# Which PSUM banks the two expert products and the token transposes share in an attention, experts and dense network kernel

## The chip, the cores and the metric

One Trainium2 chip, one core of it. The metric is the device time of one execution in microseconds (us); the kernel before is given by the median of three runs.

## What is computed

The reference is three networks in a row; only the middle one is touched by the change:

```python
x = attention(q, k, v)                  # 4 batches x 576 rows, 8 heads of 64: x is 2304 x 512
expert_idx = np.argmax(x @ w_gate, axis=1)          # one of 8 experts for each token
for e in range(E):
    xe = x[expert_idx == e]
    h = np.maximum(xe @ w1[e], 0.0)     # first product, 512 -> 1024
    ye = h @ w2[e]                      # second product, 1024 -> 512
    out[mask] = gate_w[mask, None] * ye
h = np.maximum(out @ w_in, 0.0)         # dense network, 512 -> 2048 -> 512
y = (h * h) @ w_out
```

## The kernel before

Attention runs first (to about 170 us of the span), then the experts, then the dense network. The tokens are sorted by expert with indirect DMAs, and the experts are worked in order of size: expert 0 is the largest, expert 7 the smallest, with at most 384, 384, 352, 352, 304, 256, 256 and 224 tokens. Two blocks of expert 0 are worked early, under the end of attention. Below, "expert 1" is the second in this order.

Every fp32 number is carried as two fp16 halves, so each product has three passes. For one expert, with `n` tokens:

- **First product** (`s1`, L789 to L799): eight groups, here called group 0 to group 7, one for each 128 of the 1024 hidden features. A group is 12 matmuls into one PSUM bank (L795 to L797). It is evicted in two steps: ScalarE (ACT) writes the high half of the ReLU (L798), then VectorE (DVE) reads the bank again and writes the low half (L799). The bank is free after that second step.
- **Turns** (`turn`, L989, and `transpose_x`, L782): the gathered token rows of the NEXT expert are transposed, up to 128 rows at a time, by eight TensorE transposes into one bank (L786), and copied out by ACT (L787). An expert has two or three turns, called turn 0 to turn 2. They are issued after groups 3, 5 and 7.
- **Second product** (`s2`, L840 to L856): four accumulators, one bank each, 96 matmuls in all (L849 to L851), over the eight hidden groups. At the end ACT copies the four banks into `yT` (L854).

While an expert runs, its engines also make ready what comes later. The weights of the next expert come by DMA in chunks of 128x1024 fp32, and each is split in two fp16 halves by ACT (L769) and DVE (L770). The dense network's weights are decoded and split in steps (`wide`): L871 to L873, L894 to L897 and L903 or L919 on DVE, L902 or L918 on ACT.

PSUM has eight banks of 128x512 fp32. The pool gives them to four tags of two banks each, a, b, c and d. A new tile of a tag takes one of its two banks, and its first matmul waits until the tile that held that bank has been read out. The tags before the change:

- first product: a, b, a, b, ... by group (L791);
- turns: d (L784);
- second product: c, c, a, b for its four accumulators (L843);
- the dense network's banks (`bank`, L1161): a, b, c in turn, or a and b alone while `self.narrow` is true, which it is in expert 6's second product and from the fourth of nine blocks of the dense network on (L1054, L1416). In expert 7 the first seven products of the dense network (`wide1(0, 0)`, L1058) run ahead of the second product, with a, b and c.

Each engine executes its own list of instructions in order. The recording layer (Tile) sets these lists: it reorders what the code issues by its own priorities, puts the semaphore waits in, and picks which of a tag's two banks a tile gets. A change of tags therefore moves instructions on all engines.

## Time and profile before

| what | us |
|---|---|
| median of three runs | 748.76 (748.24 to 751.16) |
| the profiled execution | 754.0, of which its span is 752.2 |
| PE (TensorE) busy | 711.6, 95% of the span |
| DVE busy | 594.4, 79% |
| ACT busy | 442.9, 59% |
| POOL busy | 212.0, 28% |

The profile comes from one execution. "PE busy" counts matmuls whose ends are modelled, and back-to-back matmuls overlap in it, so a wait shows better in the idle time before an instruction than in the busy share. "Idle before <-X" names the instruction whose end released the waiting one.

### The profile page before, as it was taken

To read this page: it belongs to the slowest core of one execution; us is meant where nothing else is said; L and a number is where in the kernel's file an instruction comes from. 1 tells how busy PE (TensorE), PEld (TensorE's weight loads), DVE (VectorE), ACT (ScalarE), POOL (GpSimd) and SP (SyncE) were. 2 spreads that over 40 slices of the span, in tenths; PEclk is the share of its full clock that TensorE was granted. 3 is DMA by queue.
4 is the path that set the end of the run, shared out by engine and by line. 5 is a ranking of instruction groups with operands and counts; after the bars stand their busy time and mean duration, and the time that the engine had idled before them with its cause. 6 is when DMAs were issued, how large, how long until landed. Compare 5 with 4: busy or idle time off the path is not lost. (4 is left out here: it accounts for less than half of the span.)

```text
span 752.2 us, 19605 instructions
## 1 busy us (share of the span) xinstructions
PE 711.6 (95%) x7979; PEld 600.8 (80%) x7979; DVE 594.4 (79%) x1454; ACT 442.9 (59%) x748; POOL 212.0 (28%) x247
## 2 busy tenths in 40 slices
PE   5989899999988999999899999999999999999996
PEld 5889799788755666788798566777899999999995
DVE  5888788864788999969987987868678787878672
ACT  5878788852466655657544342435657575757561
POOL 4493522335353401000000346533411111111011
PEclk9999999989999999999999999999999999999998
DMA  8798203765899887467713000000000000000000
GB/s 329 289 379 186 80 30 53 294 152 178 221 300 319 281 264 233 131 212 239 233 48 127 17 16 15 2 30 1 30 2 30 2 30 2 30 2 30 2 30 29
DMA packets 35656, 91.71 MB, mean 122 GB/s; under 512 B 5209, under 2 KB 13547, under 8 KB 35547
## 3 DMA queue, kind: packets, MB, share of 16 engines
q1 hardware_dynamic: 29803, 75.77, 31.6%
q0 software_dynamic: 5760, 14.65, 5.9%
q8 instruction: 64, 1.05, 0.6%
q14 instruction: 29, 0.24, 0.1%
HBM read 77.54 MB, written 13.04 MB: 120 GB/s over the span
## 5 line engine op out<-in xcount | busy, mean ns | idle before, releaser
L1178 PEld LDWEIGHTS <-wi 128*128 128x128 f16 x3024 | 170.6, 98 | 4.3 <-issue 3.1
L1315 PEld LDWEIGHTS <-wr 128*128 128x128 f16 x1008 | 98.1, 98 | 12.1 <-issue 0.7
L1201 ACT CAST wr<-work 128x1024 f16<-128x1024 f32 (+1 forms) x72 | 59.9, 832 | 58.3 <-DVE work L1207 41.6
L1178 PE MATMUL ps_a<-work,wi 128*128 128x128 f16 x1344 | 84.2, 219 | 0.0
L1178 PE MATMUL ps_b<-work,wi 128*128 128x128 f16 x1272 | 79.7, 219 | 0.4 <-ACTq L1066 0.4
L1202 DVE TENSOR_TENSOR wr<-work,wr 128x1024 f16<-128x1024 f32 (+1 forms) x72 | 70.3, 1000 | 4.4 <-ACT wr L1201 4.4
L310 PE MATMUL ps_a<-yT,wr 128*128 128x192 f32 (+2 forms) x288 | 64.9, 346 | 6.9 <-DMA wr<-in_q_dram 4.8
L322 ACT ACTIVATE pb<-pb,nm 128x192 f32<-128x192 f32 (+2 forms) x144 | 56.1, 433 | 14.8 <-DVE nm L315 14.1
L1343 POOL DMA_INDIRECT out_dram<-o,oid x18 | 25.6, 1423 | 101.4 <-ACT o L1341 66.8
L769 ACT ACTIVATE wr<-rw 128x1024 f16<-128x1024 f32 x40 | 42.2, 1057 | 19.5 <-DMA rw<-in_w_dram 18.9
L1278 POOL TENSOR_TENSOR yT<-wr 128x512 f32<-128x512 f16 x8 | 11.2, 1401 | 148.3 <-ACTq L1066 117.1
L310 PEld LDWEIGHTS ps_a<-yT,wr 128*128 128x128 f32 x288 | 45.6, 200 | 8.2 <-DMA yT<-in_k_dram 7.0
L315 DVE CUSTOM_DVE_ANT_0 pb<-ps_a,bias 128x192 f32<-128x192 f32 (+2 forms) x144 | 44.1, 326 | 9.9 <-PE ps_a L310 7.8
L770 DVE SCALAR_TENSOR_TENSOR wr<-rw,wr 128x1024 f16<-128x1024 f32 x40 | 48.8, 1220 | 3.6 <-ACT wr L769 3.4
L1210 ACT ACTIVATE work<-work 128x1024 f32<-128x1024 f32 x24 | 25.4, 1058 | 37.7 <-DVE work L1198 37.7
L333 PE MATMUL ps_b<-cst,pb 128*128 128x128 f32 x256 | 43.9, 283 | 0.7 <-ACT pts L337 0.7
L795 PE MATMUL ps_a<-work,wr 128*128 128x352 f16 (+4 forms) x112 | 33.7, 301 | 5.4 <-ACT yT L854 3.9
L778 POOL DMA_INDIRECT xg<-xd,idx x21 | 25.8, 1227 | 36.8 <-PE ps_d L786 27.7
L849 PE MATMUL ps_c<-work,wr 128*128 128x352 f16 (+5 forms) x128 | 35.9, 283 | 0.3 <-DVE work L1198 0.3
L851 PE MATMUL ps_c<-work,wr 128*128 128x352 f16 (+5 forms) x128 | 35.9, 283 | 0.0
L850 PE MATMUL ps_c<-work,wr 128*128 128x352 f16 (+5 forms) x128 | 35.9, 283 | 0.0
L1227 DVE TENSOR_TENSOR work<-work 128x512 f32<-128x512 f32 x18 | 13.0, 725 | 28.7 <-ACT work L1195 28.7
(308 smaller groups left out, 2009.5 us busy)
## 6 DMA issues: line engine op xcount, KB each, us to landing
rw<-in_w_dram SPq DMA_DIRECT2D x40, 512.0 KB
wi<-in_w_dram SPq DMA_DIRECT2D x20, 512.0 KB
rw<-in_wo_dram SPq DMA_DIRECT2D x16, 512.0 KB
rw<-in_wi_dram SPq DMA_DIRECT2D x32, 256.0 KB
wr<-in_q_dram SPq DMA_DIRECT2D x14, 512.0 KB
xd<-xhl POOLq DMA_DIRECT2D x16, 256.0 KB
yT<-in_k_dram SPq DMA_DIRECT2D x7, 576.0 KB
rw<-in_v_dram SPq DMA_DIRECT2D x12, 325.0 KB
```

The source lines that it names most:

```text
L310: nc.tensor.matmul(ps[:, s, first:hi], q[g, u, hh // 4][:, hh % 4, s if u < 4 else 0, :], self.kt[g, hh // 2][:, hh % 2, key0:key0 + hi - ...
L315: self.last_ttr = nc.vector.tensor_tensor_reduce(out=pb[:, s, first:hi], in0=ps[:, s, first:hi], in1=self.bias[:, hh, first - lo:192], sca ...
L322: self.last_exp = nc.scalar.activation(pb[:, s, first:hi], pb[:, s, first:hi], AF.Exp, bias=nm[:, s:s + 1], scale=-1.0)
L333: nc.tensor.transpose(pt[:, t, :, s, :], pb[:, s, t * P:(t + 1) * P], self.idf)
L769: self.nc.scalar.activation(t[:, 0], st, AF.Copy, scale=sc)
L770: self.nc.vector.scalar_tensor_tensor(t[:, 1], st, sc, t[:, 0], op0=ALU.mult, op1=ALU.subtract)
L849: nc.tensor.matmul(py, wh, hh, start=fc == 0, stop=False)
L850: nc.tensor.matmul(py, wl, hh, start=False, stop=False)
L1178: self.nc.tensor.matmul(ps[:, j], w[:, kp, a, w0 * P:(w0 + 1) * P], v[:, 2 * x + kp], start=kp + b == 0, stop=kp == 1 and b == 2)
L1201: self.end_act = self.fin_act = nc.scalar.copy(hi, src)
L1202: self.end_dve = self.fin_dve = V.tensor_tensor(lo, src, hi, op=ALU.subtract)
L1315: nc.tensor.matmul(ps[n], x[:, v, j], y[j][:, w], start=m + i + j == 0, stop=m == 1 and i == 2 and j == 3)
```

## The change

Three edits. The second product takes its accumulators from c, c, d, d. The turns take the banks of the first product: turn 0 from b, turn 1 from a, turn 2 from b. The dense network's products in expert 7 stay on a and b, and the dense network's own stage starts again with a, b and c.

```diff
-    def transpose_x(self, xg, dst, copy=None):
+    def transpose_x(self, xg, dst, copy=None, tag='d'):
         n = xg.shape[0]
-        pt = self.psum("d", [P, 8, P], F16)[:, :, :n]
+        pt = self.psum(tag, [P, 8, P], F16)[:, :, :n]
...
     def s2(self, ws, hts, at, n, then=None):
-        ys = [self.psum(t, [P, n]) for t in "ccab"]
+        ys = [self.psum(t, [P, n]) for t in "ccdd"]
...
-                self.transpose_x(g, xt[:, :, c * P:c * P + g.shape[0]], nc.scalar.copy)
+                self.transpose_x(g, xt[:, :, c * P:c * P + g.shape[0]], nc.scalar.copy, 'bab'[c])
...
-            self.narrow = e == 6
+            self.narrow = e >= 6
...
         nrm = {1: self.norm(1, 7168, None)}
+        self.narrow = False
         next(nrm[1])
```

How the instructions stand after it, at the two places on which the prediction rests.

On PE in expert 4 (groups of 304 tokens), the first matmuls that wait, before the change. In order: group 0, group 2, group 3, turn 0, group 4, group 5, turn 1, group 6, group 7:

```order
L795 MATMUL ps_a<-work,wr 128x304 [waits Activation_49]
...
L795 MATMUL ps_a<-work,wr 128x304 [waits Activation_49]
...
L795 MATMUL ps_b<-work,wr 128x304 [waits Activation_49]
...
L786 MATMUL ps_d<-id_131,xg 128x128 [waits PE_49]
...
L795 MATMUL ps_a<-work,wr 128x304 [waits DVE_49]
...
L795 MATMUL ps_b<-work,wr 128x304 [waits DVE_49]
...
L786 MATMUL ps_d<-id_131,xg 128x128 [waits PE_49]
...
L795 MATMUL ps_a<-work,wr 128x304 [waits DVE_49]
...
L795 MATMUL ps_b<-work,wr 128x304 [waits DVE_49]
```

The same place after it: group 0, group 1, turn 0, group 5, group 6, group 7:

```order
L795 MATMUL ps_a<-work,wr 128x304 [waits Activation_49]
...
L795 MATMUL ps_b<-work,wr 128x304 [waits PE_49]
...
L786 MATMUL ps_b<-id_131,xg 128x128 [waits DVE_49]
...
L795 MATMUL ps_b<-work,wr 128x304 [waits DVE_49]
...
L795 MATMUL ps_a<-work,wr 128x304 [waits DVE_49]
...
L795 MATMUL ps_b<-work,wr 128x304 [waits Activation_49]
```

Groups 2 and 3 wait for nothing now, and turn 0, which had a bank of its own, waits for DVE. By the bank that each gets, turn 0 waits for group 1's second eviction step, group 5 for group 3's, group 6 for group 4's, and group 7 for ACT's copy of turn 0. Before, groups 4, 5, 6 and 7 waited for groups 0, 1, 2 and 3. Experts 2, 5 and 6 are like expert 4; experts 1, 2 and 3 also have a turn 2, which waits for group 5's. In experts 1 and 3 the layer gives group 5 the bank of turn 0, so that it waits for ACT's copy; in expert 1 group 6 in the same way gets the bank of turn 1.

On DVE in expert 1 (384 tokens), a stretch of the difference, from group 3's eviction on:

```order
 L919 SCALAR_TENSOR_TENSOR wi_3346<-dec,wi_3346 128x512
+L799 SCALAR_TENSOR_TENSOR work<-ps_b,work 128x384
 L799 SCALAR_TENSOR_TENSOR work<-ps_a,work 128x384
+L871 TENSOR_SCALAR dec<-rw 128x512
 L770 SCALAR_TENSOR_TENSOR wr<-wi_3343,wr 128x1024
-L871 TENSOR_SCALAR dec<-rw 128x512
+L872 SCALAR_TENSOR_TENSOR dec<-rw,dec 128x512
 L799 SCALAR_TENSOR_TENSOR work<-ps_b,work 128x384
-L872 SCALAR_TENSOR_TENSOR dec<-rw,dec 128x512
+L873 SCALAR_TENSOR_TENSOR dec<-rw,dec 128x512
```

Group 3's low half (the first L799 row) stood six rows earlier, ahead of three weight splits (L770), and now stands behind them. In experts 2, 3 and 4 some evictions move in this way by one to four rows; from expert 5 on DVE's list is the same as before.

## Rows read from the trace of the kernel before

**Rows 1.** Busy time by stage: experts 1 to 7, one row each, from group 0 on.

```profile
core 0: us, PE busy (x) PEld busy (x) DVE busy (x) ACT busy (x) POOL busy (x), PEclk, DMA share, GB/s
197.00:235.70 38.70, 34.33 (x221) 20.72 (x219) 30.12 (x47) 20.79 (x32) 18.28 (x23) 0.96 0.91 302
235.70:269.50 33.80, 31.68 (x217) 20.61 (x216) 32.37 (x67) 22.79 (x33) 9.91 (x10) 0.95 0.86 283
269.50:301.10 31.60, 30.12 (x218) 19.85 (x216) 29.06 (x53) 18.82 (x29) 3.92 (x3) 1.00 0.79 245
301.10:326.90 25.80, 25.80 (x210) 19.67 (x208) 21.27 (x37) 15.99 (x25) 0.00 (x0) 1.00 0.41 134
326.90:350.10 23.20, 22.20 (x211) 19.73 (x209) 17.66 (x31) 13.53 (x23) 0.00 (x0) 1.00 0.77 245
350.10:376.30 26.20, 22.78 (x220) 19.86 (x218) 25.09 (x47) 16.22 (x29) 0.00 (x0) 1.00 0.75 238
376.30:404.80 28.50, 28.16 (x362) 27.64 (x360) 25.79 (x45) 11.83 (x26) 0.00 (x0) 1.00 0.09 29
```

**Rows 2.** Who PE waited for, 150 to 410 us: total, times, longest.

```profile
PE ps_a L795 <- ACT yT L854: 3.9, 3, 2.1
PE ps_d L786 <- DMA xg<-xd,idx: 3.4, 1, 3.4
PE ps_a L1131 <- DVE sd L1126: 2.3, 1, 2.3
PE ps_a L795 <- DVE work L799: 1.5, 2, 0.8
PE ps_b L849 <- DVE work L799: 1.3, 2, 1.0
PE ps_c L849 <- DVE work L1198: 0.3, 1, 0.3
```

**Rows 3.** PE's order of time in expert 2: group 2, turn 0, second product's first matmul.

```profile
241.55 0.31 PE L795 MATMUL ps_a<-work,wr 128*128 128x352 f16 x1 [2.12 <-ACT yT L854]
...
246.81 0.61 PE L786 MATMUL ps_d<-id,xg 128*128 128x128 f16 x8
...
255.20 0.32 PE L849 MATMUL ps_c<-work,wr 128*128 128x352 f16 x1
```

**Rows 4.** The stretch behind that wait; columns as in rows 1.

```profile
241.50:247.00 5.50, 5.45 (x28) 3.14 (x28) 5.50 (x17) 4.01 (x7) 2.88 (x3) 0.69 0.79 256
```

**Rows 5.** DVE's evictions L799: expert 2's group 1; group 4 of experts 2 to 6.

```profile
246.86 0.52 DVE L799 SCALAR_TENSOR_TENSOR work<-ps_b,work 128x352 f16<-128x352 f32 x1
...
252.77 0.51 DVE L799 SCALAR_TENSOR_TENSOR work<-ps_a,work 128x352 f16<-128x352 f32 x1
...
284.13 0.52 DVE L799 SCALAR_TENSOR_TENSOR work<-ps_a,work 128x352 f16<-128x352 f32 x1
...
313.54 0.47 DVE L799 SCALAR_TENSOR_TENSOR work<-ps_a,work 128x304 f16<-128x304 f32 x1
...
339.26 0.42 DVE L799 SCALAR_TENSOR_TENSOR work<-ps_a,work 128x256 f16<-128x256 f32 x1
...
362.56 0.42 DVE L799 SCALAR_TENSOR_TENSOR work<-ps_a,work 128x256 f16<-128x256 f32 x1
```

**Rows 6.** PE: the first matmul of group 6 in experts 1 to 6.

```profile
214.66 0.33 PE L795 MATMUL ps_a<-work,wr 128*128 128x384 f16 x1
...
251.28 0.31 PE L795 MATMUL ps_a<-work,wr 128*128 128x352 f16 x1
...
282.80 0.31 PE L795 MATMUL ps_a<-work,wr 128*128 128x352 f16 x1
...
311.42 0.29 PE L795 MATMUL ps_a<-work,wr 128*128 128x304 f16 x1
...
336.50 0.27 PE L795 MATMUL ps_a<-work,wr 128*128 128x256 f16 x1
...
360.23 0.27 PE L795 MATMUL ps_a<-work,wr 128*128 128x256 f16 x1
```

**Rows 7.** ACT: the copy of turn 1 in expert 1.

```profile
217.48 1.00 ACT L787 COPY work<-ps_d 128x1024 f16<-128x1024 f16 x1
```

## The prediction

> **What bounds the kernel now.** I read the stage table first, then the list of PE's waits, then the order of time on PE, DVE and ACT around those waits. The change touches experts 0 to 7, and of these experts 1 to 6 carry the price. In the stage table [rows 1] the reader is to see how full DVE is beside PE: it is busy for 30.12 of 38.70 us in expert 1 (78%), 96% in expert 2, 92% in expert 3, 82% in expert 4, 76% in expert 5 and 96% in expert 6. PE runs most of these stages without a pause, but no engine has much room.

> The list of waits [rows 2] is to show what the two edits can remove. PE stands 3.9 us, in three pieces, before a group of the first product until ACT has copied an accumulator of the second product out of a bank of tag a (L854). It stands 1.3 us, in two pieces, in the second product until DVE has evicted a group of the first (L849 behind L799). The 3.4 us for the gathered rows, the 2.3 us for the norm's small matrices (L1126) and the 1.5 us of L795 behind L799 have other causes and are not removed. The order of time shows the largest piece: group 2 of expert 2 starts at 241.55 after 2.12 us [rows 3].

> **What goes.** With accumulators in c and d, both kinds of wait lose their cause: 3.9 + 1.3 = 5.2 us. One piece has a tail. [...] Groups 2 and 3 took 246.81 - 241.55 = 5.26 us [rows 3], while groups 6 and 7 of the same expert, with a turn of some 0.36 us, took 255.20 - 251.28 = 3.92 us [rows 3, 6], 1.78 a group. The tail cost 5.26 - 3.56 = 1.7 us. So the credit is 5.2 us, or 6.9 with the tail.

> [...] I leave tails out of the sum, since expert 3, which holds the second piece of the 3.9 us, stands at a clock of 1.00 throughout [rows 1].

> **What comes in its place.** The turns no longer have banks of their own. A turn and two groups share a pair of banks, and the distance between a bank's use and its next use shrinks. Before, group 6 needed group 2's eviction, with groups 3, 4, 5 and two turns in between. Now it needs group 4's, with only group 5 and turn 1 in between, some 2 us. Likewise turn 0 needs group 1's, group 5 needs group 3's.

> How late are evictions? Rows 5 give DVE's time for group 4 in experts 2 to 6 and rows 6 the start of group 6. The eviction of group 4 ends at 253.28, 284.65, 314.01, 339.68 and 362.98 (start plus duration); group 6 started at 251.28, 282.80, 311.42, 336.50 and 360.23 [rows 5, 6]. If DVE's list ran at the same times, group 6 would start later by 2.0, 1.85, 2.6, 3.2 and 2.75 us. What follows it on PE (group 7, turn 2, the second product) would move with it, because each of those is ready on time.

> In expert 1, group 6 gets the bank of turn 1 and needs ACT's copy of it, which ends at 217.48 + 1.00 = 218.48 [rows 7] against a start at 214.66 [rows 6]: 3.8 us. The new order has nine matmuls of the second product ahead of group 6. At 0.16 us each they fill 1.5 us of that, so 2.3 is left; 1.0 of it is the longest piece of the second product's own wait [rows 2], which is no longer met there. I take 1.3.

> The removed waits do not return as credit in these figures. In expert 2, group 2 may start 2.12 us earlier, but turn 0 then needs group 1's eviction, which ends at 246.86 + 0.52 = 247.38 [rows 5], and turn 0 started at 246.81 [rows 3]. The gap moves from group 2 to turn 0. Behind it stand the same groups and the same tail. The late one after ACT's copies is DVE.

> **The smaller parts.** In expert 0, the transposes of its last block now wait for ACT's copy of an accumulator of tag d, and an eviction stands behind the copy of a turn; such a copy takes 1.00 us [rows 7], so the two cost at most 2. They are hidden: expert 1's turn 0 waits 3.4 us for a gather [rows 2], whose DMA does not depend on PE there. Without that cover they would cost those 2 us. In expert 7, the dense network's seven products have four banks for six. The wait of 0.3 us for a bank of tag c goes [rows 2], and two products come just behind an eviction of the first product; I take -0.3, with 0 to +1 as the other end. On POOL and on SP's queue only gathers and loads that are early by many us change places with their neighbours: nothing.

> **The sum.** Its ends lie far apart, because a lag of PE need not reach the end of its stage, nor the next one.
> - Upper end: every lag is passed on in full. 1.3 + 2.0 + 1.85 + 2.6 + 3.2 + 2.75 = 13.7 us.
> - Lower end: no lag, credit alone: -5.2, with the tail -6.9.
> - The value: a lag is passed on where DVE's list itself waits for PE, since then the next evictions and weight splits are late as well. DVE's share says where that is. In experts 2, 3 and 6 (96, 92 and 96%) DVE goes on with weights whatever PE does and finds PE's groups waiting: a lag there is caught up, as DVE sets the stage's end. In experts 1, 4 and 5 (78, 82 and 76%) it has room, waits, and carries the lag on: 1.3 + 2.6 + 3.2 = 7.1. Expert 6 gives some back: PE's 2.3 us on the norm [rows 2] shrink when PE comes later. I take 2.1 of them, near all, as DVE is at 96% there and does not move with PE: 7.1 - 2.1 = 5.0. The 0.3 of expert 7 stays inside that figure's error.

> The profiled execution took 754.0 us with a span of 752.2; the sum makes it 759.0. That execution is 5.2 us above the median of the runs shown, so on the median, 748.8, the change gives **753.8 us**, 0.7% slower.

> **The rivals.**
> 1. *The lags never arise* (faster). Without waits at groups 2 and 3, PE hands its first groups over earlier, ACT and DVE evict earlier, and the short distance is enough. It gives 748.8 - 5.2 = 743.6. It decides where group 4's eviction ends within some 2 us of the group's end. For it: the copies L854 no longer hold anything up. Against it: in expert 4, which had no wait of that kind, the eviction still came 2.6 us too late for the new distance. [...] Chance 0.18.
> 2. *All is caught up* (no change). DVE and the weight loads set the end of each stage, so PE's new waits only fill time in which it would have waited at the next place. For it: three stages with DVE above 90%. Against it: experts 4 and 5. Removing 1, 4 and 5 but for 0.5 gives 749.3. Chance 0.27.
> 3. *Every lag adds up*, with the moved evictions on DVE (group 3's of expert 1 now behind three weight splits) on top of nothing else: 748.8 + 13.7 = 762.5, if DVE waits for PE in all stages. Against it: the shares of 92 to 96%. Chance 0.10.

> My forecast has 0.45, of which 0.05 lies within the bound of no change.

> **How the numbers follow.** About 0.5% (3.7 us) is what a measurement of this kernel can tell from no change. Slower by more: 0.40 + 0.10 = 0.50. Within: 0.27 + 0.05 = 0.32. Faster by more: 0.18. The range of 8 in 10 runs from 744.5 to 760.5: below lies about half of rival 1, above most of rival 3. As cases of both signs hold much of the chance, the forecast's own range is 751.5 to 757.5.

> **What would show it.** In the list of PE's waits after the change, L795 behind L854 and L849 behind L799 are gone. In their place stand L786 and L795 behind DVE's L799, and some L795 behind ACT's L787, together 6 us or more between 205 and 365 us. Group 6 of experts 4 and 5 starts 2 us or more later after its group 0 than now; experts 4 and 5 last 2 to 3 us longer, and experts 2, 3 and 6 stay within 2 us of their 33.8, 31.6 and 26.2 us. From the start of expert 7 to the end the time is unchanged within 1 us. The forecast is wrong if those new waits sum to under 3 us, or if the stages after expert 6 differ.

## The result, and the profile after

The changed kernel takes 754.0 us (median; 750.6 to 757.4) against 749.3 us (745.1 to 754.3) of the kernel before in the same comparison: +4.7 us, ratio 1.0061, 95% interval 1.0045 to 1.0076. That is slower, by 3.4 to 5.7 us. The forecast was +5.0.

The two profiled executions hide it: their spans are 752.2 us before and 751.2 after. Attention, which no edit touches, happened to be faster in the second one (expert 1 starts at 197.02 before and at 191.33 after). So I compare stages, which start and end at the same instruction in both. From the start of expert 1 to the end of expert 7 it is 207.72 us before and 212.63 after, +4.9. From there to the end of the span it is 347.5 and 347.2.

The stage table of the changed kernel, experts 1 to 7, answers to [rows 1]; the columns are the same.

```profile
191.33:231.09 39.76, 34.56 (x219) 20.72 (x217) 30.81 (x49) 21.56 (x32) 19.64 (x25) 0.96 0.93 311
231.09:265.64 34.55, 31.40 (x219) 20.72 (x217) 32.99 (x69) 22.79 (x32) 11.26 (x8) 0.95 0.86 283
265.64:299.57 33.93, 31.76 (x218) 20.73 (x216) 28.52 (x51) 19.06 (x28) 3.47 (x3) 0.95 0.68 216
299.57:326.99 27.42, 26.01 (x210) 19.70 (x208) 20.74 (x33) 16.53 (x27) 0.00 (x0) 1.00 0.35 112
326.99:351.89 24.90, 22.34 (x211) 19.71 (x209) 19.63 (x34) 15.60 (x25) 0.00 (x0) 1.00 0.80 256
351.89:375.97 24.08, 22.72 (x221) 19.87 (x219) 22.40 (x43) 14.24 (x25) 0.00 (x0) 1.00 0.71 228
375.97:403.96 27.99, 27.99 (x362) 27.72 (x359) 25.52 (x45) 11.72 (x25) 0.00 (x0) 1.00 0.09 29
```

| expert | before | after | difference | forecast |
|---|---|---|---|---|
| 1 | 38.67 | 39.76 | +1.1 | +1.3 |
| 2 | 33.83 | 34.55 | +0.7 | 0 |
| 3 | 31.59 | 33.93 | +2.3 | 0 |
| 4 | 25.81 | 27.42 | +1.6 | +2.6 |
| 5 | 23.17 | 24.90 | +1.7 | +3.2 |
| 6 | 26.25 | 24.08 | -2.2 | -2.1 |
| 7 | 28.40 | 27.99 | -0.4 | -0.3 |

PE's waits, 150 to 410 us, answer to [rows 2]:

```profile
PE ps_b L786 <- DVE work L799: 6.4, 4, 3.1
PE ps_b L795 <- ACT work L787: 3.4, 2, 2.2
PE ps_a L795 <- DVE work L799: 3.4, 4, 1.3
PE ps_b L795 <- DVE work L799: 1.5, 2, 1.1
PE ps_b L1178 <- DVEq L1066: 0.9, 1, 0.9
PE ps_a L795 <- ACT work L787: 0.9, 1, 0.9
...
PE ps_a L1131 <- DVE sd L1126: 0.4, 1, 0.4
```

The waits for L854 and of L849 behind L799, 5.2 us, are gone. In their place a turn or a group waits for a bank that a group (L799) or a turn (L787) still holds: 6.4 + 3.4 + 3.4 + 1.5 + 0.9 = 15.6 us; of the kind L795 behind L799 the kernel before had 1.5 us. (`DVEq` is DVE's instruction sequencer.) Two old waits are covered now: the gathered rows (3.4) and most of the norm's 2.3.

Why is a bank late? In expert 2 it is the order of the lists. Group 1's low half (the L799 row below) stands behind weight splits and table steps, and turn 0 needs its bank. Between 231 and 242 us DVE waits only 0.4 us, so the rows ahead of the eviction are work, not waits. DVE of the changed kernel, and PE:

```profile
239.61 1.22 DVE L770 SCALAR_TENSOR_TENSOR wr<-wi,wr 128x1024 f16<-128x1024 f32 x1
240.75 0.34 DVE L705 TENSOR_REDUCE pick<-work 128x20 f32<-128x180 f32 x1
241.00 0.52 DVE L799 SCALAR_TENSOR_TENSOR work<-ps_b,work 128x352 f16<-128x352 f32 x1
...
241.57 1.01 PE L786 MATMUL ps_b<-id,xg 128*128 128x128 f16 x8 [3.15 <-DVE work L799]
```

In expert 3 it is ACT's list. ACT stands idle for 3.31 us before a step of the dense network's weights (L902) whose input DVE has not made yet. Behind that step stand group 3's high half and the copy of turn 0, whose bank group 5 needs. ACT, and PE:

```profile
275.11 0.95 ACT L902 ACTIVATE wi<-dec 128x896 f16<-128x896 f32 x1 [3.31 <-DVE dec L897]
275.97 0.45 ACT L798 ACTIVATE work<-ps_b 128x352 f16<-128x352 f32 x1
276.31 1.00 ACT L787 COPY work<-ps_b 128x1024 f16<-128x1024 f16 x1
...
277.37 0.31 PE L795 MATMUL ps_b<-work,wr 128*128 128x352 f16 x1 [2.17 <-ACT work L787]
```

So much do ACT and DVE wait inside their own lists in experts 1 to 6 of the changed kernel (191 to 376 us):

```profile
ACT wi L902 <- DVE dec L897: 17.0, 11, 3.5
ACT wr L769 <- DMA rw<-in_w_dram: 14.9, 12, 3.6
ACT wr L769 <- DMA wi<-in_w_dram: 14.0, 8, 4.3
...
DVE wr L770 <- ACT wr L769: 16.6, 12, 4.0
```

None of these rows is an eviction, but an eviction behind one of them waits too. In expert 3 the last matmul of group 3 started at 272.65 and took 0.31 us; ACT was idle from 271.80 on, and yet it started that group's high half at 275.97, behind L902. DVE's rows, too, ran in the order of the list: the stretch of it that stands with the change ran row for row, from L919 at 212.04 to the third L799 at 215.65.

### The profile page after: what moved, and what is told of

The parts are those of the page before. It is cut to its first block, busy times and chain, and to the rows that moved or that the text cites. A ratio compares the mean times of both kernels' runs of the same rounds, so it can differ in the third digit from the quotient of the medians.

```text
span 751.2 us, 19606 instructions
## 1 busy us (share of the span) xinstructions
PE 709.4 (94%) x7979; PEld 599.5 (80%) x7979; DVE 594.6 (79%) x1454; ACT 444.6 (59%) x748; POOL 214.2 (29%) x247
## 3 DMA queue, kind: packets, MB, share of 16 engines
q1 hardware_dynamic: 29803, 75.77, 31.6%
## 5 line engine op out<-in xcount | busy, mean ns | idle before, releaser
L1178 PEld LDWEIGHTS <-wi 128*128 128x128 f16 x3024 | 170.6, 98 | 4.4 <-issue 3.2
L1315 PEld LDWEIGHTS <-wr 128*128 128x128 f16 x1008 | 98.1, 98 | 12.1 <-issue 0.7
L1178 PE MATMUL ps_a<-work,wi 128*128 128x128 f16 x1344 | 84.2, 219 | 0.0
L1178 PE MATMUL ps_b<-work,wi 128*128 128x128 f16 x1320 | 82.7, 219 | 0.9 <-DVEq L1066 0.9
L322 ACT ACTIVATE pb<-pb,nm 128x192 f32<-128x192 f32 (+2 forms) x144 | 56.2, 433 | 12.5 <-DVE nm L315 11.6
L769 ACT ACTIVATE wr<-rw 128x1024 f16<-128x1024 f32 x40 | 42.2, 1057 | 23.5 <-DMA rw<-in_w_dram 16.6
L770 DVE SCALAR_TENSOR_TENSOR wr<-rw,wr 128x1024 f16<-128x1024 f32 x40 | 48.9, 1221 | 5.5 <-ACT wr L769 5.4
L1210 ACT ACTIVATE work<-work 128x1024 f32<-128x1024 f32 x24 | 25.4, 1058 | 37.9 <-DVE work L1198 37.9
L795 PE MATMUL ps_a<-work,wr 128*128 128x352 f16 (+4 forms) x112 | 33.9, 303 | 4.2 <-DVE work L799 3.4
L795 PE MATMUL ps_b<-work,wr 128*128 128x352 f16 (+4 forms) x112 | 33.1, 296 | 4.9 <-ACT work L787 3.4
L796 PEld LDWEIGHTS <-wr 128*128 128x128 f16 x224 | 22.3, 100 | 18.1 <-issue 11.2
L849 PE MATMUL ps_c<-work,wr 128*128 128x352 f16 (+5 forms) x128 | 35.9, 284 | 0.0
L851 PE MATMUL ps_d<-work,wr 128*128 128x352 f16 (+5 forms) x128 | 35.9, 284 | 0.0
```

The source lines that it names most:

```text
L322: self.last_exp = nc.scalar.activation(pb[:, s, first:hi], pb[:, s, first:hi], AF.Exp, bias=nm[:, s:s + 1], scale=-1.0)
L769: self.nc.scalar.activation(t[:, 0], st, AF.Copy, scale=sc)
L770: self.nc.vector.scalar_tensor_tensor(t[:, 1], st, sc, t[:, 0], op0=ALU.mult, op1=ALU.subtract)
L795: nc.tensor.matmul(ph, wh, xt[:, kc], start=kc == 0, stop=False)
L849: nc.tensor.matmul(py, wh, hh, start=fc == 0, stop=False)
L1178: self.nc.tensor.matmul(ps[:, j], w[:, kp, a, w0 * P:(w0 + 1) * P], v[:, 2 * x + kp], start=kp + b == 0, stop=kp == 1 and b == 2)
```

## The experiments

My theory: the loss is PE waiting for banks that turns and groups now share, because their evictions are late. Rivals: (A) the accumulators' move itself costs; (B) DVE sets each stage's end, so waits removed or added on PE count for little; (C) part of it lies in expert 7. All ratios are against the kernel before, run beside it.

**1. One edit at a time.** The accumulators alone keep the turns on d:

```diff
-    ys = [self.psum(t, [P, n]) for t in "ccab"]
+    ys = [self.psum(t, [P, n]) for t in "ccdd"]
```

> Only the accumulators move: the second product takes c, c, d, d, the turns stay on d and the dense network's flag is as before. The sharing theory (the loss of 4.7 us comes from the turns in the first product's banks): L795 behind L854 (3.9 us) and L849 behind L799 (1.3 us) are gone, no new wait for L799 comes, but in experts 1, 2 and 3 the third accumulator wants the bank of turn 2 and waits for ACT's copy of it, some 1.5 us each. Time between -5 and 0 us against the kernel before, -2 taken. Rival A (the accumulators' move is what costs, by the order it gives to DVE and ACT): +3 to +5 us. Rival B (DVE sets the stages' ends, so a wait removed is worth nothing): within 1 us of 0, with DVE at 95% or more in the stages whose wait went.

Measured: ratio 1.0035 (1.0009 to 1.0060), +3.6 us in the medians. The L854 waits are gone, and the expected new one came at the expected place, but far larger:

```profile
PE ps_d L849 <- ACT work L787: 9.4, 4, 6.2
...
PE ps_a L795 <- DVE work L799: 0.8, 2, 0.5
```

Its 6.2 us piece is in expert 2. ACT of this kernel stands idle for 4.18 us for a load of weights, with turn 2's copy (the 128x768 row) four rows behind:

```profile
252.96 1.06 ACT L769 ACTIVATE wr<-rw 128x1024 f16<-128x1024 f32 x1 [4.18 <-DMA rw<-in_w_dram]
253.93 0.45 ACT L798 ACTIVATE work<-ps_a 128x352 f16<-128x352 f32 x1
254.27 0.94 ACT L902 ACTIVATE wi<-dec 128x896 f16<-128x896 f32 x1
255.11 0.45 ACT L798 ACTIVATE work<-ps_b 128x352 f16<-128x352 f32 x1
255.45 0.80 ACT L787 COPY work<-ps_d 128x768 f16<-128x768 f16 x1
```

The time is what rival A said and not what the theory said (-5 to 0), by a mechanism that rival A did not have: here the third and fourth accumulators share the d banks with the turns. The turns alone, with the accumulators on c, c, a, b:

```diff
-    self.transpose_x(g, xt[...], nc.scalar.copy)
+    self.transpose_x(g, xt[...], nc.scalar.copy, 'bab'[c])
```

> Only the turns move, to b, a, b; the accumulators stay on c, c, a, b. The sharing theory: the waits for L854 stay near 3.9 us, the new waits of the first product and the turns for L799 and L787 come on top with some 12 to 16 us in the list of PE's waits; time +5 to +9 us against the kernel before, above the changed kernel's +4.7. Rival A (the accumulators' move costs): within 1.5 us of 0. Rival B (stages end by DVE whatever PE waits for): the same +4.7 as the changed kernel, within 1.

Measured: ratio 1.0036 (1.0015 to 1.0057), +3.4 us in the medians, below the 5 to 9 expected and nearer to rival B's +4.7. The new waits for L799 and L787 are there (3.5 + 2.8 + 2.3 + 3.6 + 0.9 = 13.1 us), but the waits for L854 do not come on top of them: 0.6 us of the 3.9 is left. Rival A, which wanted nothing here, falls. The two halves do not add up to the whole, +3.6 and +3.4 against +4.7: each kernel has its own sharing and its own lists. The dense network's flag alone:

```diff
-            self.narrow = e == 6
+            self.narrow = e >= 6
...
+        self.narrow = False
```

> Only the dense network's banks in expert 7 (a and b alone) and the reset after it. The sharing theory: nothing, within 1 us of 0; experts 1 to 6 as before, expert 7 within 0.5 us of its 28.4 us. Rival C (part of the loss comes from expert 7 and the dense network): +2 us or more, in expert 7 or in the first blocks of the dense network.

Measured: ratio 1.0016 (0.9990 to 1.0042), which can't be told from 1, but leaves room for the 2 us of rival C. The stages leave none: expert 7 took 28.00 us against 28.40, experts 1 to 7 took 206.96 against 207.72, and from there to the end it is 347.5 us in both. Rival C falls by the stages of one execution.

**2. Only turn 2 in the first product's banks.** The changed kernel, with one string edited:

```diff
-    self.transpose_x(g, xt[...], nc.scalar.copy, 'bab'[c])
+    self.transpose_x(g, xt[...], nc.scalar.copy, 'dda'[c])
```

> The changed kernel, but with turns 0 and 1 back on d and only turn 2 on a bank of the first product (a), where no later group of the same expert follows it. The sharing theory: neither the waits for L854 and L849 nor those of groups 5, 6 and 7 for L799 and L787; the accumulators on d come after turns 0 and 1 are long copied. Time -3 to -5 us against the kernel before, and 8 us under the changed kernel. Rival B (DVE sets the ends): within 1 us of 0. Rival A (the accumulators' move costs): +3 to +5 us.

Measured: ratio 0.9997 (0.9974 to 1.0020). Taking turns 0 and 1 out of a and b (turn 2 goes from b to a) takes the loss away, which shows that it comes from the sharing. But the gain of 3 to 5 us that the theory forecast did not come; within 1 us of 0 is what rival B said. PE's waits of this kernel:

```profile
PE ps_d L786 <- DMA xg<-xd,idx: 3.5, 1, 3.5
PE ps_a L795 <- DVE work L799: 3.0, 4, 0.9
PE ps_a L1131 <- DVE sd L1126: 2.6, 1, 2.6
PE ps_d L849 <- ACT work L787: 1.6, 2, 1.3
```

In experts 2 and 3, where the pieces of 2.12 and 1.48 us behind L854 went, group 2 now waits 0.83 and 0.80 us for DVE. What ACT's copies held up, DVE's evictions hold up next, though not in full: expert 2 lasts 30.86 us, 3.0 less than before, and its clock stands at 1.00. Experts 4 to 6 give 2.5 us of that back (77.71 against 75.23 us), with waits of 0.95 us for L799 and 1.29 for L787 in expert 5, and 2.58 us for the norm and a clock of 0.94 in expert 6.

**3. The bank free after ACT's step.** If DVE's second step is what holds the bank, taking the bank out of it must turn the sign of the change. Both kernels get the edit:

```diff
-    nc.vector.scalar_tensor_tensor(ht[:, 1], ph, 0.0, ht[:, 0], ...)
+    nc.vector.scalar_tensor_tensor(ht[:, 1], ht[:, 0], 0.0, ht[:, 0], ...)
```

> The changed kernel, but the low half of a group (L799) is computed from the high half in SBUF and not from the bank, so that a bank is free after ACT's step; DVE keeps the same number of instructions in its list. The low halves come out as zero, so this leaves that part of the products out. The sharing theory, with DVE's late second step as the cause: the 11.3 us in which PE waits for L799 go to under 1; the 4.3 us for ACT's copy L787 stay between 1 and 5; the 3.4 us for the gathered rows and the 2.3 us for the norm come back. Experts 1 to 6 then last 172 to 178 us in place of 184.6, and the kernel is level with its control, the kernel before with the same edit, or up to 4 us faster. Rival D (the turns cost by ACT's copies and by their place in PE's list, not by DVE): still 3 to 5 us above the control.

> The control: the kernel before with the same edit to L799, which leaves the same low halves out. The sharing theory: of its waits only the 1.5 and 1.3 us for L799 go; the 3.9 us for L854, 3.4 for the gathered rows and 2.3 for the norm stay. Experts 1 to 6 last 175 to 178 us in place of 179.3; time 1 to 4 us under the kernel before. Rival B (DVE's load sets the stages' ends): within 1 us of the kernel before, if L799 takes as long from SBUF as from the bank.

Measured: 1.0086 (1.0060 to 1.0112) with the change, 1.0133 (1.0104 to 1.0161) for its control. The sign turned: 759.3 against 763.4 us, the change now 4 us faster (the two intervals overlap slightly), with experts 1 to 7 at 214.0 and 217.4 us. The waits for L799 went to nothing in both. What nobody expected is that both kernels became slower than the kernel before. L799 takes as long as it did (517 ns for 128x352, against 519), so DVE's load is the same. The waits of the changed kernel with this edit:

```profile
PE ps_a L795 <- ACT work L798: 4.2, 3, 3.2
PE ps_b L786 <- ACT work L798: 3.8, 2, 3.1
```

ACT's high half is late now: the lists were made anew, and in this kernel ACT stands idle before L902 for 25.4 us in all, 190 to 400 us. Rival D falls (the control is slower still), and so does rival B in its plain form: with each L799 as long as before, the control lost 10.4 us. In its experts 1 to 7 PE waits 17.6 us in place of 12.7, and the clock of experts 3, 5 and 6 is 0.94 to 0.95 in place of 1.00. The pair does not single out DVE's step, though. In the changed kernel ACT holds the banks in its place (8.0 us), and the control lost more behind L854 (5.9 us, from 3.9) and behind L798; the sign turned by both.

**4. The place in the list.** Two edits that are meant to move nothing but the order. Priority for the two eviction steps:

```diff
-    nc.scalar.activation(ht[:, 0], ph, AF.Relu)
+    with self.tc.high_priority(): nc.scalar.activation(ht[:, 0], ph, AF.Relu)
```

and the same for L799.

> The changed kernel, with the two eviction steps L798 and L799 given priority when the lists are made, so that they stand some rows earlier in ACT's and DVE's lists; no work is added or left out. If the evictions are late because of what stands ahead of them in DVE's list: PE's waits for L799 fall from 11.3 to under 6 us and the time by 2 to 4 us, to a ratio of 1.000 to 1.004 against the kernel before. If they are late because DVE is full (rival B): waits and time within 1 us of the changed kernel's, ratio 1.005 to 1.008.

Measured: ratio 1.0022 (0.9998 to 1.0045); experts 1 to 7 take 208.35 us, where the changed kernel took 212.63. The time is as expected, the reason is not: L799's waits only fell to 9.8 us (5.1 + 2.8 + 1.9). It was the 4.3 us behind L787 that went. Then ordering edges, by which a weight split or a dense-network step that the code issues behind an eviction stays behind it:

```diff
+        with self.after_ev():
             self.nc.scalar.activation(t[:, 0], st, AF.Copy, scale=sc)
             self.nc.vector.scalar_tensor_tensor(t[:, 1], st, sc, t[:, 0], ...)
```

and so around both parts of `wide`; `after_ev` puts what is inside behind the last L798 on ACT and the last L799 on DVE.

> The changed kernel with an ordering edge on ACT and on DVE: a weight split (L769, L770) and a step of the dense network's weights (L871 to L919) that the code issues behind a group's eviction stays behind it in the lists too. No work is added or left out. Theory (evictions are late because of rows that stand ahead of them in ACT's and DVE's lists and themselves wait for a DMA or for the other engine, not because an engine is full): PE's waits for L799 and L787 fall from 15.6 to under 5 us between 190 and 400; experts 1 to 7 last 205 to 209 us in place of 212.6; ratio to the kernel before 0.995 to 1.001. Rival E (the engines are full, so the splits that now come later make the next expert's weights late): new waits for L769 or L770 on PE and a ratio of 1.004 or more.

> The control: the kernel before with the same ordering edges. Theory: its waits for L854 (3.9 us) shrink, as ACT's copies no longer stand behind splits, but less than the sharing kernel's shrink; the time is 0 to 3 us under the kernel before, and the changed kernel with the same edges (after_order) is within 2 us of it, in place of 4.7 above. Rival E: slower than the kernel before by 2 us or more, with waits for L769 or L770 on PE.

Measured: 1.0078 (1.0056 to 1.0101), and 0.9995 (0.9976 to 1.0014) for the control. Experts 1 to 7 last 206.1 us with the change, as expected, and 209.9 without; expert 2's turn 0 waits 1.04 us in place of 3.15. The waits for L799 and L787 fell from 15.6 to 8.0 us, not under 5. The total says the opposite of what the theory said: the changed kernel with the edges is 6.4 us above its control. The gain is given back at one place, the dense network's start. (Lines stand 8 to 12 lower in this kernel and in the last two below: L794 is L786, L795 is L787, L803 is L795, L807 is L799, L857 is L849, L1143 is L1131, L1190 is L1178. L1078 is the branch at the head of `overflow`, which DVE reaches only after its list of expert 7.)

```profile
PE ps_b L1190 <- DVEq L1078: 5.9, 1, 5.9
PE ps_b L794 <- DVE work L807: 3.8, 3, 2.0
PE ps_a L1143 <- DVE sd L1138: 2.3, 1, 2.3
PE ps_a L803 <- DVE work L807: 2.8, 5, 0.9
```

From the end of expert 7 to the end this kernel takes 353.9 us, where the changed kernel takes 347.2. Counted from the start of expert 1, PE passes that branch after 212.0 us here and after 213.6 in the changed kernel: 6.5 us less in the experts are 1.6 us at the branch. From the start of expert 1 to the end of expert 7 DVE was busy for 176.3 us here, and for 180.9 in turn2_a, which took as long (206.6 us) without the edges: they put some 4.6 us of its work off, up to where PE then waits. Rival E's ratio came, but not its waits for weights (L769 or L770) on PE.

**5. Toward a version that beats both.** Turn 2 alone on a, as in 2 (turn2_a); the second product two hidden groups at a time, first for accumulators 0 and 1, then for 2 and 3, so that the d banks are wanted 6 matmuls later; and either the priority or the edges of 4:

```diff
-    for fc in range(8):
+    for fc, ds in [(f, d) for g in range(0, 8, 2) for d in ((0, 1), (2, 3)) for f in (g, g + 1)]:
...
-        for d, py in enumerate(ys):
+        for d, py in [(d, ys[d]) for d in ds]:
...
```

> Turns 0 and 1 on d, turn 2 on a (as in turn2_a), with two more edits: the second product works two hidden groups for its first two accumulators and then for its last two, so that the banks of tag d are wanted 12 matmuls (1.9 us) after its start and not 6; and L798 and L799 have priority in the lists. The theory (PE's time is its work plus its waits for banks): the 1.6 us for L787 and 3.2 us for L799 that turn2_a had go to under 1.5 together; left are the gathered rows (3.5) and the norm (2.6). Time 3 to 6 us under the kernel before, ratio 0.992 to 0.996. Rival B: within 1 us of it.

Measured: 1.0004 (0.9984 to 1.0025). The waits for L787 went, those for L799 are still 6.6 us. The gain of 3 to 6 us did not come; the time is again rival B's.

> Turns 0 and 1 on d, turn 2 on a, the second product two hidden groups at a time for two accumulators (as in turn2_skew_prio), and the ordering edges in place of the priority. Theory: L799 waits fall from 6.6 us to under 2.5; left are the gathered rows (3.5), the norm (2.3 to 4); ratio to the kernel before 0.992 to 0.998. Rival E: waits for L769 or L770 on PE and a ratio of 1.000 or more.

Measured: 1.0030 (1.0014 to 1.0046): rival E's time, without its waits for weights on PE. Experts 2 to 5 run without any wait, which tells what PE's own work in them is. The stage table of this kernel, experts 2 to 5:

```profile
231.16:261.04 29.88, 29.88 (x219) 20.02 (x216) 27.41 (x58) 18.86 (x29) 9.22 (x8) 1.00 0.87 284
261.04:290.98 29.94, 29.94 (x218) 19.86 (x216) 23.65 (x40) 17.66 (x27) 2.87 (x3) 1.00 0.67 220
290.98:316.68 25.70, 25.70 (x211) 19.68 (x209) 21.48 (x36) 16.84 (x26) 0.00 (x0) 1.00 0.52 169
316.68:338.53 21.85, 21.85 (x211) 19.68 (x208) 18.69 (x35) 13.50 (x21) 0.00 (x0) 1.00 0.52 178
```

Against the kernel before these four stages save 33.83 + 31.59 + 25.81 + 23.17 - 107.37 = 7.0 us. Then experts 6 and 7 take 3.4 us more than before, with a wait of 3.6 us for the norm, and PE again waits 5.9 us at the dense network's start. The last kernel drops the edges from expert 6 on and moves expert 1's turns behind the gather:

```diff
-        if self.ev_a is not None:
+        if self.ev_a is not None and self.expert < 6:
...
-                if fc in (3, 5, 7) and more:
-                    turn(nxt, e + 1, fc // 2 - 1)
+                if fc in ((5, 6, 7) if e == 1 else (3, 5, 7)) and more:
+                    turn(nxt, e + 1, fc - 5 if e == 1 else fc // 2 - 1)
```

> What the runs point to, put together: turns 0 and 1 on d and turn 2 on a, the second product two hidden groups at a time for two accumulators, the ordering edges up to expert 5 alone (in expert 6, expert 7 and the dense network the lists are as in the changed kernel), and in expert 1 the three turns one group pair later, after groups 5, 6 and 7, so that PE does not stand before turn 0 until the rows are gathered. Theory: experts 2 to 5 as in turn2_skew_order (29.9, 29.9, 25.7, 21.9 us), expert 1 some 3 to 5 us under 38.7, expert 7 back at 28.0, and the dense network's first wait (5.9 us there) back under 1. Ratio to the kernel before 0.986 to 0.995. Rival E (the splits that come later make something else late): 0.998 or more, with a new wait in expert 6 or at the dense network's start.

Measured: 1.0113 (1.0087 to 1.0139), rival E. Experts 2 to 5 are as expected (29.88, 29.95, 25.69, 21.85 us); expert 1 did not gain, since turn 2 now waits 4.6 us for a bank (L794 below). Experts 6 and 7 take 7.1 us more than before, and the dense network's start waits again:

```profile
PE ps_b L1190 <- DVEq L1078: 5.5, 1, 5.5
PE ps_a L1143 <- DVE sd L1138: 4.9, 1, 4.9
PE ps_a L794 <- DVE work L807: 4.6, 1, 4.6
PE ps_d L857 <- ACT work L795: 2.2, 1, 2.2
```

In the stretch before the dense network's start, in the columns of [rows 1], DVE is busy for 27.37 of 28.90 us and has next to no room to catch up. From the start of expert 1 to the end of expert 7 it was busy for 177.4 us (176.9 in the run before this one), against 181.3 in the kernel before:

```profile
375.00:403.90 28.90, 23.07 (x310) 22.65 (x307) 27.37 (x44) 11.76 (x22) 1.44 (x1) 0.98 0.17 56
```

No version beat the kernel before. The nearest (0.9995, 0.9997 and 1.0004, of before_order, turn2_a and turn2_skew_prio) are level with it.

## Why the prediction was right

- **The removed waits, and no credit for them.** Right for this change. Both kinds are gone. As the text said for expert 2, the gap moved from group 2 to turn 0, and it grew from 2.12 to 3.15 us. It is the sharing that takes the credit there: without it, in experiment 2, expert 2 did gain 3.0 us.
- **The new waits.** Right in kind and place: 15.6 us, of them 12.5 between 205 and 365 us, where at least 6 were asked for. All stand before turns or before groups 4 to 7 behind L799 or L787.
- **Expert 1.** The figure fits (+1.3 forecast, +1.1 measured), the sum behind it does not, so this is luck. The text priced one new wait, at group 6, and let the 3.4 us for the gathered rows stand. Group 6 waited 0.88 us, but group 4, turn 0 and group 5 waited 1.28, 1.83 and 1.21 us as well, while the wait for the gather went.
- **Experts 4 and 5.** Right in sign, too large: 2.6 and 3.2 us were forecast, 1.6 and 1.7 came. Only a part of it came at group 6 (1.02 us in expert 4, 0.40 in expert 5); the rest came at group 5 and, in expert 5, at turn 0, and two old waits of expert 5 (0.68 and 0.33 us) went. The step took DVE's old times for group 4's eviction as fixed. They were not: counted from the stage's start, group 6 could start some 1.0 us earlier than that in both. The reason given, that DVE "waits, and carries the lag on" where its list "itself waits for PE", is not in the rows. In these two experts of the kernel before (301.1 to 350.1 us) DVE waited for ACT and for a DMA, never for PE:

```profile
DVE wr L770 <- ACT wr L769: 6.7, 4, 3.9
DVE wi L903 <- ACT wi L902: 2.4, 3, 1.0
DVE dec L871 <- DMA rw<-in_wi_dram: 0.7, 2, 0.5
```

ACT's splits L769 in turn waited 10.5 us there for weight loads. In expert 5, where DVE's list is the same before and after, its 3.9 us wait for such a split ended 4.91 us after the stage's start before and 3.76 us after. So the sign and the order of size were right, and why the lag is passed on was not.
- **Expert 3.** This is the step that failed: "In experts 2, 3 and 6 ... DVE goes on with weights whatever PE does", so a lag there is caught up. It cost 2.3 us. Nor was it the wait that was priced and then struck out, 1.85 us at group 6 behind DVE: it stands at group 5, behind ACT's copy of turn 0, a wait that the section on the change names and the sum has no term for. These stages last as long as PE works in them, plus PE's waits, plus what a lower clock costs. With 29.94 us of PE's own work (experiment 5), expert 3 lasts 33.93 = 29.94 + 2.17 of waiting + 1.8 of lower clock. Expert 2 lasts 34.55 = 29.88 + 3.15 + 1.5. A busy share of 92% does not say that evictions pass at once: they stand in a list behind rows that work (expert 2) or wait themselves (expert 3). The two errors, 2.5 us too much in experts 4 and 5 and 3.1 too little in 2 and 3, nearly cancelled. That the total came within 0.3 us of the forecast is luck to that extent. Of the prediction's own signs, these stage figures miss four: experts 4 and 5 were to last 2 to 3 us longer (1.6 and 1.7), and experts 3 and 6 to stay within 2 us (+2.3 and -2.2, the latter as its own sum had it).
- **Expert 6, expert 7, and after.** Right in the sum: PE's wait for the norm shrank from 2.3 to 0.4 us and the stage by 2.2; expert 7 by 0.4; after it 0.3 us of difference.
- **The tails.** A tail is work at a lower granted clock behind a wait, as in [rows 4]. Left out of the sum, and there: expert 3's clock fell from 1.00 to 0.95. The longer of the new waits (3.15 and 2.17 us, and the 1.83 in expert 1, with a clock of 0.52 over 203.37 to 205.00) each brought a tail; those of 1.0 to 1.1 us in experts 4 and 5 did not, and the clock stayed at 1.00 there.
- **Rivals.** That the lags never arise fell by the 15.6 us; even with the evictions ordered first half of them stayed (8.0 us). That all is caught up fell for this change, but it named the time of two versions (experiment 2 and the first of 5). DVE's load as such does not hold those two at the dense network's start: they come to it after 206.6 and 206.4 us of experts 1 to 7, against 207.7 before, and wait 0.9 us there. The 5.5 to 5.9 us came only in three kernels with ordering edges, which put DVE's work off. That every lag adds up fell by the 2.2 us of expert 6 and the covered wait for the gather.

What stays open: how much of DVE's work in experts 6 and 7 would have to go elsewhere before a kernel without bank waits is faster was not tried. Why priority for L798 and L799 took away the waits behind L787 and left most of those behind L799 is not shown.

## What to carry to other kernels

- When two uses share a ring of banks, ask what stands ahead of the evicting instruction in its engine's list, and what THAT waits for. Here ACT stood idle for 46 us in six stages before rows that wanted weights or DVE, and evictions that were ready sat behind some of them; the busy share shows none of it. The longest wait, in expert 2, came from rows that did work.
- Compare stages that begin and end at the same instruction, not spans: here one stretch that no edit touches differed by as much as the effect.
- An order that takes waits off the bounding engine puts other work off; ask where that work comes due. Seven us saved in four stages came back: 3.4 in the next two, and 5.9 as a wait at one branch.

## What the hardware showed

```profile
278.26 0.31 PE L795 MATMUL ps_b<-work,wr 128*128 128x352 f16 x1
278.41 0.39 PE L796 MATMUL ps_b<-work,wr 128*128 128x352 f16 x1
278.59 0.50 PE L797 MATMUL ps_b<-work,wr 128*128 128x352 f16 x1
278.88 0.50 PE L795 MATMUL ps_b<-work,wr 128*128 128x352 f16 x1
```

The granted clock is 1.00 over 265.64 to 278.40, with the wait in it, and 0.63 over 278.40 to 283.00. A wait of 2.17 us thus cost some 4.0 us of the stage (33.93 - 29.94).

It did not always fall so late, and in these cases the length of the wait does not tell. After the 3.15 us in expert 2 turn 0 ran slowly at once: it took 1.01 us, with a clock of 0.50 over 241.57 to 242.37, where the next turn of equal size, at 246.95, took 0.61, with a clock of 1.00 over 246.95 to 247.39. After 3.66 us at the same place in the kernel with priority (experiment 4) it took 0.61, and the matmuls of 128x352 behind it took 0.31 us at first and 0.50 only from 243.67 on.
